# HGRN2 attention and a PReLU network on one core: a first step gated by batch, sooner keys, a wait inside the state increments, and a new hand-written order of work

## The chip, the cores and the metric

The kernel runs on one core of a Trainium2 chip. TensorE (PE) multiplies, with its weight loads listed apart (PEld); VectorE (DVE) and ScalarE (ACT) do the elementwise work, GpSimd (POOL) some setup, and SyncE (SP) issues most DMAs. PSUM takes the products, SBUF holds everything else. The metric is the device time of one execution, in microseconds.

## The reference

Two blocks, one after the other. First a gated linear attention: batch 4, 8 heads, 768 time steps, head size 48. The second block is a two-layer network with a PReLU between its layers: 3072 tokens (batch by time), 384 to 2048 to 384.

```
f = 1.0 / (1.0 + np.exp(-f_logit))
for t in range(S):
    state = f[:, :, t, :, None] * state + np.einsum('bhd,bhe->bhde', k[:, :, t], v[:, :, t])
    y[:, :, t] = np.einsum('bhd,bhde->bhe', q[:, :, t], state)
x = y.transpose(0, 2, 1, 3).reshape(B * S, H * D)
h = x @ w_in
g = np.maximum(h, 0.0) + alpha * np.minimum(h, 0.0)
out = g @ w_out
```

All of it is float32. Weights arrive as 64-bit words and are put together on the chip.

## The kernel before

**Steps.** The time axis is cut into 6 chunks of 128 and the batch into 2 pairs, so there are 12 steps (`steps`, L776): step n is chunk c = n // 2 of batch pair bp = n % 2. In a step a chunk's attention for two batches and eight heads is computed, and then the network for those 256 tokens. Only the state (kept in rows of `vs`) links the steps of a batch pair.

**Stages.** Each piece of work is a Python generator, one letter per kind. A line of text, `ORDER`, names which generator goes on next; each call to it issues instructions up to its next `yield`. `manual_schedule` (L784) keeps that order on PE, DVE, ACT and SP. POOL is not in that list. START writes the order out for the first part (until step 5), USUAL is repeated after that, with T S Y O for step n, P and K with a plus for step n + 1, and n for the network of step n - 1. `X:3` means three turns.

- P, `prepare` (L267), 8 turns: (1) loads of f, q, k and v (on POOL for steps 1 to 4, on SP for the others), (2) sigmoid on f and copies on ACT, (3) the products of decays kr and fs, and the lagged queries qd (`lagged`, L297), on DVE, (4) ACT's us copies; for later chunks two scans; for the first chunk q4 and k4 (L338, L364), (5) more decayed queries (for later chunks q4, k4 and the first of them), (6) and (7) keys decayed to the end of a block (`ended`, `keys`), transposed by DVE into kt, and queries decayed from its start, (8) ACT's A copies (L445).
- S and T, `scores` (L549) of batch 0 and 1 of the pair, 4 turns: first products on PE, masked copies on DVE (L572), second products (k4 by us) on PE, masked copies (L582).
- K, `keys_moved` (L449): 16 DMAs bring the transposed keys kt into ksn, 8 issued by SP and 8 by POOL.
- M, `landed` (L460): a small matmul that reads ksn, and so waits for these DMAs on PE. It writes into a network bank, which `network` then takes as its next ph (named pw; `early`, L658).
- O, `carry` (L466), 4 turns (8 in the first chunk): "off" products on PE (L495), ACT copies, the state increments on PE (L526, 64 matmuls of ksn by vs into the PSUM tile pairs[1]), and `moved(0)` on DVE (L536, L540), which brings the state on. The first chunk also has "half" products (L480), PE transposes for ksn and ACT copies.
- Y, `attend` (L601), 4 turns (5 in step 0): A copies on ACT (two turns, L606), the output products py on PE (L617), then y copies on ACT, `moved(1)` on DVE and ten DMAs into xT (step 0: products xt, L636, instead of DMAs).
- n, `network` (L653), 13 turns (12 in step 0): eight ph groups f0 to f7 (12 matmuls, a relu on ACT at L669 and two gates on DVE at L671; sums on DVE after f3 and f7), then the second layer in seven half-size products pa to pe (16 matmuls each): turn 9 has pa and pb, 10 pc and pd, 11 more of pa and pc, 12 pe and the store of o1, 13 the store of o0. Step 0 uses plain products po instead (turns 9 to 12).
- a, w: the eight pieces of w_in, upper part on ACT (two operations, and a load on SP) and the rest on DVE. b, g: the same for w_out. W: sums of the halves of w_out on DVE. i: a matmul on constants that fills a pause on PE. X: gives PSUM banks to the network.

**Buffers that matter.** f, q, k, us, k4, kt and ksn exist once, so a load waits until the last reader of the step before. pairs[0] and pairs[1] are two PSUM tiles of two banks, used by S, T, O and Y in turn; the network has four banks.

Of the kernel before, what the change touches and what calls it, by code (L numbers as in the profile page):

```python
# [8 lines left out]
F32 = mybir.dt.float32  # L9
# [5 lines left out]
AF = mybir.ActivationFunctionType  # L15
# [13 lines left out]

BEGUN = 5  # L30
START = (
# [7 lines left out]
)  # L39
USUAL = "T S T S n:4 T S P+ T S P+ n:2 Y M n O:4 n:2 P+ Y P+ Y P+ Y n:3 P+:3 K+ n"  # L40

LOOSE = ("a", "w", "b", "g", "W", "i", "X")

# [17 lines left out]
def kernel(  # L61
# [72 lines left out]
    def bank(name):  # L134
        return net["pool"].tile([128, 512], F32, tag="net", name=name)
# [131 lines left out]
    def prepare(bp, c, x):  # L267
# [5 lines left out]

        def load(name, src, bufs=2):
            t = work.tile([128, W], F32, tag=name, name=f"{name}_{i}", bufs=bufs)
            loads.dma_start(out=t.rearrange("p (u x) -> p u x", u=U),
                              in_=src[b0:b0 + U, c].rearrange("u p h t -> p u (h t)"))
            return t

        f = quads(load("f", fT, 1))  # L280
# [5 lines left out]
            loads.dma_start(out=vs[bp][t_, cc, :, 0:DM], in_=v[b0:b0 + U, c, t_].rearrange("u t d -> t u d"))  # L286
        yield

        nc.scalar.activation(f, f, AF.Sigmoid)
        nc.scalar.copy(kr[:, :, 2:3], f[:, :, 3:4])  # L290
        qdv = [qd[:, :, QO[d]:QO[d] + NB * (4 - d)].rearrange("p g (i r) -> p g i r", r=4 - d) for d in range(4)]
        nc.scalar.copy(qd[:, :, 0:DB], q.rearrange("p (g t) -> p g t", t=DB))
# [6 lines left out]
            nc.vector.tensor_tensor(qdv[d], last[:, :, :, 1:5 - d],  # L299
                                    f[:, :, 1:5 - d].rearrange("p (g i) r -> p g i r", i=NB), ALU.mult)  # L300

        nc.vector.tensor_tensor(kr[:, :, 1:2], f[:, :, 2:3], f[:, :, 3:4], ALU.mult)
        lagged(1)
        nc.vector.tensor_tensor(kr[:, :, 0:1], f[:, :, 1:2], kr[:, :, 1:2], ALU.mult)
        lagged(2)
        nc.vector.tensor_tensor(fq, f[:, :, 0:1].rearrange(by32, i=NB), kr[:, :, 0:1].rearrange(by32, i=NB), ALU.mult)
        lagged(3)
        yield


# [24 lines left out]
        if c:  # L335
            scans()
            yield
        nc.vector.tensor_tensor(q4, q4, f[:, :, 0:1].rearrange("p (g i) o -> p g i o", i=NB)  # L338
                                .broadcast_to((128, G, NB, 4)), ALU.mult)
        pre = ps[:, 0:NS - 1].rearrange("p (g i) -> p g i", i=NB + 1)  # L340
# [22 lines left out]
        k4 = x["k4"] = work.tile([128, W], F32, tag="k4", name=f"k4_{i}", bufs=1)  # L363
        nc.vector.tensor_tensor(k4, k, kr.rearrange("p n r -> p (n r)"), ALU.mult)  # L364
        if c:
            earlier(2)
        else:
# [92 lines left out]
    def landed(bp, c, x):  # L460
        to = early[steps[steps.index((bp, c)) - 1]] = bank(f"pw_{bp}_{c}")
        nc.tensor.matmul(to[:, 0:4], lhsT=ident, rhs=x["ksn"][:, 0, 0:128:32], start=True, stop=True,
                         skip_group_check=True)
        yield

    def carry(bp, c, x):  # L466

        i = f"{bp}_{c}"
        home = more if (bp, c) == steps[0] else pairs
        off = home[0]  # L470
        if not c:
            half = home[1]
            for u in range(U):
                for hp in range(HP):
                    for j in range(NJ):
                        g = (u * HP + hp) * NJ + j
                        o = (u * HP + hp) * 16
                        for par in range(2):
                            r_ = rows(par)
                            nc.tensor.matmul(half[DB * j:DB * (j + 1), par, o:o + 16], lhsT=x["k16"][r_, g],  # L480
                                             rhs=x["q16"][r_, g], start=True, stop=True)
# [36 lines left out]
        pd = home[1]  # L518
        ksn = x["ksn"]
        for u in range(U):  # L520
# [24 lines left out]
        yield  # L545
        moved(0)
        yield
# [105 lines left out]
    def network(bp, c, x):  # L653
# [1 line left out]
        xT = x["T"]  # L655
        plain = (bp, c) == steps[0]
        for f in range(NH):
            ph = early.pop((bp, c), None)  # L658
            if ph is None:
                ph = bank(f"ph{f}_{i}")  # L660
            tiles = (2 * f, 2 * f + 1) if plain else (f, f + NH)
            for kt in range(NK):
                for j, m in enumerate(tiles):
# [10 lines left out]
                sums(slice(f - 3, f + 1))  # L674
            yield

        def store(u, o):
            t0 = ((U * bp + u) * NC + c) * C
            nc.sync.dma_start(out=out[t0:t0 + C], in_=o)

        if plain:
            po = [bank(f"po{u}_{i}") for u in range(U)]
# [39 lines left out]
        product(pc, s3, t3, more=True)  # L722
        plus(o0[:, DH:DM], pd, u2)
        nc.scalar.activation(o0[:, 0:DH], pa[:, 0:DH], AF.Copy, scale=UP)
        yield
        pe = bank(f"pe_{i}")
        product(pe, s4, b22)
# [3 lines left out]
        store(1, o1)  # L731
        yield
        plus(o0[:, DH:DM], pe, o0[:, DH:DM])
        store(0, o0)
        yield

    late, early = {}, {}

    def sums(fs_):

# [43 lines left out]
    with tc.manual_schedule(engines={mybir.EngineType.PE, mybir.EngineType.DVE, mybir.EngineType.Activation,  # L784
                                     mybir.EngineType.SP}):
        run = {}
        for n, step in enumerate(steps):
            x = {}
            for key, stage_ in zip("POYKMn", (prepare, carry, attend, keys_moved, landed, network)):
# [59 lines left out]
```

## Time and profile before

| what | value |
|---|---|
| median of 3 executions | 616.25 us (614.02 to 617.06) |
| the profiled execution, its own time | 616.97 us |
| its span | 615.2 us |
| PE busy | 586.0 us |
| PEld busy | 523.2 us |
| DVE busy | 495.1 us |
| ACT busy | 243.6 us |
| POOL busy | 84.4 us |
| mean granted TensorE clock | 0.97 |

The span is the time from the first to the last instruction that the profile shows; 1.77 us of the profiled execution's time lie outside it. Busy time is summed over an engine's instructions, and a matmul's end is modelled, so a busy PE is a full queue and not PE at its peak. A view of waits lists what ended an engine's idle time; a chain of waits goes back from the last instruction to whatever released it. The granted clock is the share of TensorE's full clock that the throttle let through.

The costliest groups are the first layer's matmuls and the gate on DVE (line, engine, operation, output and inputs, count, busy us and mean ns, idle before):

```
L664 PE MATMUL ph<-xT,w_in_sb 128*128 128x256 f32 x1032 | 231.5, 382 | 0.0
L671 DVE SCALAR_TENSOR_TENSOR gate<-neg,om,ph 128x256 f32<-128x256 f32 x172 | 72.9, 478 | 37.8 <-ACT neg L669 37.8
```

### The profile page before, as it was taken

Reading aid. Unit: us, or ns where it says so; the run is one execution under the profiler, and the core shown is the slowest. Engines: PE = TensorE matmul, PEld = TensorE weight load, DVE = VectorE, ACT = ScalarE, POOL = GpSimd, SP = SyncE. Lnnn points to the kernel's source line nnn. Section 1 sums busy time; section 2 is a strip of 40 time slices with the busy share of each in tenths; the row PEclk is TensorE's granted clock in tenths of the full one; section 3 lists DMA queues with packets and bytes.
Section 4 is the critical chain, followed back from the end, with each engine's and each line's share of the span. In section 5 each row is a group of like instructions: output and inputs, shape, how many; then the busy total and the mean of one; then the engine's idle time right before and its main releaser. Section 6 shows DMA issues by size and latency. Waiting matters only on the chain.

```text
span 615.2 us, 18129 instructions
## 1 busy us (share of the span) xinstructions
PE 586.0 (95%) x7762; PEld 523.2 (85%) x7762; DVE 495.1 (80%) x997; ACT 243.6 (40%) x418; POOL 84.4 (14%) x162
## 2 busy tenths in 40 slices
PE   2689999999999699999999999999999999999997
PEld 1468857899899599899899899889889889889997
DVE  7869999999788679688988988988988986982351
ACT  4588863434431352342442442343343343231110
POOL 9110004004003001200200300200200200200000
PEclk7688999999999799999999999999999999999999
DMA  9937616114105301601601511501511511201000
GB/s 306 344 106 260 236 29 144 36 35 120 23 1 158 49 2 28 180 3 33 161 16 27 161 23 27 165 19 27 141 43 27 140 43 28 52 2 28 26 1 26
DMA packets 52720, 50.36 MB, mean 82 GB/s; under 512 B 26688, under 2 KB 43200, under 8 KB 52640
## 3 DMA queue, kind: packets, MB, share of 16 engines
q1 hardware_dynamic: 42624, 37.46, 20.6%
q0 software_dynamic: 5504, 9.90, 6.4%
q10 hardware_dynamic: 4512, 1.85, 1.3%
q8 instruction: 61, 1.00, 0.7%
q14 instruction: 19, 0.16, 0.1%
HBM read 36.21 MB, written 4.72 MB: 67 GB/s over the span
## 4 chain that ended last, share of the span: by engine, by line
PE 92%; DMA 2%; issue 2%; DVE 2%; ACT 1%; SPq 0%; DVEq 0%
PE ph L664 36%; PE pc L703 10%; PE pa L703 9%; PE pair L563 6%; PE pw L664 5%; PE pd L703 5%; PE pb L703 5%; PE pe L703 4%; PE pair L617 4%; PE po L684 3%; DMA k<-in_kT 1%; PE pair L526 1%; PE pair L495 1%; PE more L773 1%; PE xt L636 1%
## 5 line engine op out<-in xcount | busy, mean ns | idle before, releaser
L664 PE MATMUL ph<-xT,w_in_sb 128*128 128x256 f32 x1032 | 231.5, 382 | 0.0
L664 PEld LDWEIGHTS ph<-xT,w_in_sb 128*128 128x128 f32 x1032 | 193.9, 190 | 28.5 <-issue 1.7
L671 DVE SCALAR_TENSOR_TENSOR gate<-neg,om,ph 128x256 f32<-128x256 f32 x172 | 72.9, 478 | 37.8 <-ACT neg L669 37.8
L669 ACT ACTIVATE neg<-ph 128x512 f32<-128x512 f32 x86 | 50.1, 595 | 118.8 <-PE ph L664 78.0
L703 PE MATMUL pc<-t,S 128*128 128x192 f32 x352 | 61.5, 328 | 0.0
L703 PE MATMUL pa<-w_out_sb,gate 128*128 128x192 f32 x352 | 61.2, 327 | 0.0
L703 PEld LDWEIGHTS pa<-w_out_sb,gate 128*128 128x128 f32 x352 | 57.9, 190 | 0.8
L455 POOL DMA_DIRECT2D ksn<-kt x80 | 46.1, 584 | 87.8 <-DVE kt L407 62.0
L703 PEld LDWEIGHTS pc<-t,S 128*128 128x128 f32 x352 | 57.2, 190 | 0.6
L445 ACT COPY A<-q 48x512 f32<-48x512 f32 x44 | 27.2, 617 | 66.2 <-DVE q L393 65.8
L647 POOL DMA_DIRECT2D xT<-y x22 | 11.8, 543 | 286.7 <-ACT y L624 286.7
L572 DVE COPY_PREDICATED ad<-mraw,pair 128x256 f32<-128x256 int32 (+1 forms) x96 | 41.3, 451 | 5.2 <-PE pair L563 2.2
L582 DVE COPY_PREDICATED ad<-mquad,pair 128x224 f32<-128x224 int32 (+6 forms) x140 | 41.1, 299 | 4.2
L347 DVE TENSOR_TENSOR us<-us,fs 128x768 f32<-128x768 f32 (+5 forms) x60 | 37.0, 616 | 0.8
L707 DVE SCALAR_TENSOR_TENSOR Csum<-pc,Csum 128x192 f32<-128x192 f32 x22 | 7.9, 358 | 36.9 <-PE pc L703 36.6
L606 ACT COPY A<-ad 32x512 f32<-32x512 f32 x48 | 29.5, 615 | 10.8 <-DVE ad L582 10.4
L326 ACT COPY us<-qd 128x256 f32<-128x256 f32 x48 | 29.5, 673 | 10.6 <-DVE qd L299 10.3
L664 PE MATMUL pw<-xT,w_in_sb 128*128 128x256 f32 x120 | 31.0, 412 | 0.0
L748 DVE TENSOR_TENSOR S<-gate 128x512 f32<-128x512 f32 x44 | 30.3, 688 | 0.8
L703 PE MATMUL pe<-w_out_sb,S 128*128 128x192 f32 x176 | 30.5, 327 | 0.0
L703 PE MATMUL pb<-t,gate 128*128 128x192 f32 x176 | 30.4, 326 | 0.0
L703 PE MATMUL pd<-w_out_sb,S 128*128 128x192 f32 x176 | 30.4, 326 | 0.0
(125 smaller groups left out, 792.0 us busy)
## 6 DMA issues: line engine op xcount, KB each, us to landing
w_out_raw<-in_w_out SPq DMA_DIRECT2D x8, 767.8 KB, 5.9
w_in_raw<-in_w_in SPq DMA_DIRECT2D x8, 767.2 KB, 9.8
out<-o SPq DMA_DIRECT2D x24, 192.0 KB, 2.0
f<-in_fT SPq DMA_DIRECT2D x8, 512.0 KB, 3.9
q<-in_qT SPq DMA_DIRECT2D x8, 512.0 KB, 4.8
k<-in_kT SPq DMA_DIRECT2D x8, 512.0 KB, 6.5
vs<-in_v SPq DMA_DIRECT2D x16, 192.0 KB, 6.6
ksn<-kt SPq DMA_DIRECT2D x80, 32.0 KB, 2.2
```

The source lines that it names most:

```text
L326: nc.scalar.copy(q4[:, :, :, r], qdv[r][:, :, :, 0])
L347: nc.vector.tensor_tensor(us[:, :, UO[m]:UO[m] + 4 * n].rearrange("p g (i r) -> p g i r", r=4), us[:, :, skip:skip + 4 * n].rearrange("p g ...
L455: (nc.gpsimd if a % 2 else nc.sync).dma_start(out=ksn[32 * b:32 * (b + 1)].rearrange("p u (h x) -> p (u h) x", h=HP)[:, :, 32 * a:32 * a + n],
L563: nc.tensor.matmul(to[DB * j:DB * (j + 1), par, hp * step + lo:hp * step + hi], lhsT=keys[r_, g * DB:(g + 1) * DB], rhs=by[r_, g, lo:hi], ...
L572: nc.vector.copy_predicated(adu[:, :, :, d:4], mraw[:, d, :, d:4].bitcast(I32).unsqueeze(1).broadcast_to((128, H, NB, n)), rv[:, :, QO[d]: ...
L582: nc.vector.copy_predicated(ad[:, u, :, :, 4 * m:DB], mquad[:, lo:lo + n].bitcast(I32).unsqueeze(1).unsqueeze(1).broadcast_to((128, 2, HP, ...
L606: nc.scalar.copy(A[s_].rearrange("p u h t -> p (u h) t")[:, :, s_], ad[s_].rearrange("p u r h t -> p (u r h) t"))
L664: nc.tensor.matmul(ph[:, j * T:(j + 1) * T], lhsT=w_in_sb[:, kt, m * 128:(m + 1) * 128], rhs=xT[:, kt], start=(kt == 0 and j == 0), stop=( ...
L669: nc.scalar.activation(neg, phv, AF.Relu, scale=-1.0)
L671: nc.vector.scalar_tensor_tensor(gate[:, m % NH, m // NH], neg[:, j], om[:, m:m + 1], phv[:, j], ALU.mult, ALU.add)
L703: nc.tensor.matmul(to[:, 0:DH], lhsT=of(f), rhs=by(f), start=(f == 0 and not more), stop=(f == NH - 1), skip_group_check=True)
L748: nc.vector.tensor_tensor(to, x_, y_, op)
```

## The change

- In step 0, f is loaded in two DMAs, one per batch of the pair, and sigmoid and kr's first product are done in two halves. The lagged queries of step 0 come behind kr and fs instead of between them.
- k4 is computed ahead of q4, at the top of turn 4 or 5 of P, instead of after it.
- `landed` and `early` are gone. In `carry`, two small matmuls per later chunk (64 rows each, into four unused columns of pairs[1]) read ksn just ahead of the state increments.
- In the last step, the store of o0 is cut into two halves of the columns; the left half is issued in turn 11 of n, the right half in turn 13.
- START and USUAL are new. In USUAL, both first products stand together, py comes behind pc and pd, moved(0) behind the lags and scans of the next step, and the key moves one turn ahead of P's last.

```
--- before.py
+++ after.py
@@ -29,15 +29,15 @@
 
 BEGUN = 5
 START = (
-    "i P0 i P0:2 i P0:3 O0:2 a T0 P0 T0 i S0 i S0 i P1 T0 a P0 P1 O0 P1 O0 S0 T0 S0 i O0 P1 O0 S1 P1 Y0 i "
-    "O0:2 i Y0 w O1:2 Y0 S1 a Y0 X a S1 T1 a Y0 T1 w P2:2 T1 w P1 w:2 a:2 T1 w P1 S1 n0 a n0 b w:2 b g b "
-    "n0:2 O1 n0 O1 b P2 O1 g Y1 O1 n0:2 g n0 b Y1 S2 g P2 T2 b T2 n0 g:2 b S2 n0 g b g W O1 W P1 P2 n0 P2 "
-    "O1 Y1:2 P2 W n0 T2 S2 P3 S2 n1 P3 T2 Y2 K2 P3 n1 W n1 Y2 n1:2 O2 T3 n1 T3 M2 n1 W O2 n1 P3 S3 O2 S3 "
-    "O2 n1 P3 n1 P2 Y2 P3 n1 Y2 P4 P3 P4 P3 n1 S3 P4 T3 n1 n2 S3 n2:2 T3 Y3 n2 K3 n2:2 M3 n2 O3:2 P4 O3 "
-    "n2 O3 P4:2 n2:2 Y3:3 n2 S4 T4 P4 n2:2 T4 S4 n3 P5 K4 n3 P4 P5 S4:2 T4:2 n3 P5 M4 n3:4 O4 Y4 O4 Y4 "
-    "O4:2 n3 P5:2 n3:2 Y4 P5:2 Y4 n3:2 K5 n3 P5 "
+    "i P0:3 S0 i P0:2 T0 i O0:2 a i P0:2 P1 i T0 i:3 O0 T0 O0 P1 S0 P1 S0 O0 T0 S0 i w P0 i P1 O0 P1 O0 i "
+    "Y0:2 O0 a S1 Y0 O1 Y0 O1 X a S1 w Y0 T1 P2 T1 w a:2 w P1 n0 a:2 P1 w a w S1 P2 S1 n0 T1 w P1 w b "
+    "n0:2 T1 O1 b g O1 P2 b Y1 g n0 b n0 g O1 n0 b g b g n0 O1 P2 b:2 g n0 S2 P2 Y1 g:2 O1 S2 W P2 n0:2 "
+    "O1 P2 Y1:2 W n0 S2 W T2 P2 P3:2 S2 T2 W n1:2 T2 O2 T2 W P3 Y2 K2 n1 Y2 O2 n1:3 T3 S3:2 n1 T3 n1:2 "
+    "O2:2 P3:2 n1 Y2 P3 Y2 P3 n1 O3 n1 O3 S3 P4 T3 n1 P4 T3 P3 n2 S3 P4 Y3 n2 K3 Y3 n2:3 O3 P4 O3 n2 P4 "
+    "n2:2 Y3 n2 P4 n2 Y3 T4 P4 S4 T4 P5 S4 P4 n2:2 T4 S4 T4 S4 Y4 n2 n3:2 P5 n3:3 K4 Y4 O4:3 P5:2 O4 n3:3 "
+    "Y4 P5 n3:2 Y4 P5 n3 P5:2 n3 K5 n3 "
 )
-USUAL = "T S T S n:4 T S P+ T S P+ n:2 Y M n O:4 n:2 P+ Y P+ Y P+ Y n:3 P+:3 K+ n"
+USUAL = "S:2 T:2 n:3 P+ n S P+ T S n:3 T n Y n O P+ O P+ O Y n O P+ Y:2 n:2 P+:2 K+ n P+"
 
 LOOSE = ("a", "w", "b", "g", "W", "i", "X")
 
@@ -273,8 +273,10 @@
 
         def load(name, src, bufs=2):
             t = work.tile([128, W], F32, tag=name, name=f"{name}_{i}", bufs=bufs)
-            loads.dma_start(out=t.rearrange("p (u x) -> p u x", u=U),
-                              in_=src[b0:b0 + U, c].rearrange("u p h t -> p u (h t)"))
+            tu = t.rearrange("p (u x) -> p u x", u=U)
+            parts = [slice(u, u + 1) for u in range(U)] if name == "f" and not ahead else [slice(0, U)]
+            for p in parts:
+                loads.dma_start(out=tu[:, p], in_=src[b0:b0 + U, c].rearrange("u p h t -> p u (h t)")[:, p])
             return t
 
         f = quads(load("f", fT, 1))
@@ -286,7 +288,9 @@
             loads.dma_start(out=vs[bp][t_, cc, :, 0:DM], in_=v[b0:b0 + U, c, t_].rearrange("u t d -> t u d"))
         yield
 
-        nc.scalar.activation(f, f, AF.Sigmoid)
+        by_u = [slice(u * G * NB // U, (u + 1) * G * NB // U) for u in range(U)] if not ahead else [slice(0, G * NB)]
+        for p in by_u:
+            nc.scalar.activation(f[:, p], f[:, p], AF.Sigmoid)
         nc.scalar.copy(kr[:, :, 2:3], f[:, :, 3:4])
         qdv = [qd[:, :, QO[d]:QO[d] + NB * (4 - d)].rearrange("p g (i r) -> p g i r", r=4 - d) for d in range(4)]
         nc.scalar.copy(qd[:, :, 0:DB], q.rearrange("p (g t) -> p g t", t=DB))
@@ -299,12 +303,16 @@
             nc.vector.tensor_tensor(qdv[d], last[:, :, :, 1:5 - d],
                                     f[:, :, 1:5 - d].rearrange("p (g i) r -> p g i r", i=NB), ALU.mult)
 
-        nc.vector.tensor_tensor(kr[:, :, 1:2], f[:, :, 2:3], f[:, :, 3:4], ALU.mult)
-        lagged(1)
+        for p in by_u:
+            nc.vector.tensor_tensor(kr[:, p, 1:2], f[:, p, 2:3], f[:, p, 3:4], ALU.mult)
+        if ahead:
+            lagged(1)
         nc.vector.tensor_tensor(kr[:, :, 0:1], f[:, :, 1:2], kr[:, :, 1:2], ALU.mult)
-        lagged(2)
+        if ahead:
+            lagged(2)
         nc.vector.tensor_tensor(fq, f[:, :, 0:1].rearrange(by32, i=NB), kr[:, :, 0:1].rearrange(by32, i=NB), ALU.mult)
-        lagged(3)
+        for d in range(3 if ahead else 1, 4):
+            lagged(d)
         yield
 
 
@@ -335,6 +343,8 @@
         if c:
             scans()
             yield
+        k4 = x["k4"] = work.tile([128, W], F32, tag="k4", name=f"k4_{i}", bufs=1)
+        nc.vector.tensor_tensor(k4, k, kr.rearrange("p n r -> p (n r)"), ALU.mult)
         nc.vector.tensor_tensor(q4, q4, f[:, :, 0:1].rearrange("p (g i) o -> p g i o", i=NB)
                                 .broadcast_to((128, G, NB, 4)), ALU.mult)
         pre = ps[:, 0:NS - 1].rearrange("p (g i) -> p g i", i=NB + 1)
@@ -360,8 +370,6 @@
                 by = fq[:, :, 1:NB:NQ]
             nc.vector.tensor_tensor(to, of, by.unsqueeze(3).broadcast_to((128, G, 2, 4)), ALU.mult)
 
-        k4 = x["k4"] = work.tile([128, W], F32, tag="k4", name=f"k4_{i}", bufs=1)
-        nc.vector.tensor_tensor(k4, k, kr.rearrange("p n r -> p (n r)"), ALU.mult)
         if c:
             earlier(2)
         else:
@@ -457,12 +465,6 @@
                     in_=kt[32 * a:32 * (a + 1)].rearrange("p (g b x) -> p g b x", b=NJ, x=32)[:, :, b, 0:n])
         yield
 
-    def landed(bp, c, x):
-        to = early[steps[steps.index((bp, c)) - 1]] = bank(f"pw_{bp}_{c}")
-        nc.tensor.matmul(to[:, 0:4], lhsT=ident, rhs=x["ksn"][:, 0, 0:128:32], start=True, stop=True,
-                         skip_group_check=True)
-        yield
-
     def carry(bp, c, x):
 
         i = f"{bp}_{c}"
@@ -517,6 +519,10 @@
         yield
         pd = home[1]
         ksn = x["ksn"]
+        if c:
+            for par in range(2):
+                r_ = slice(64 * par, 64 * par + 64)
+                nc.tensor.matmul(pd[r_, par, 508:512], lhsT=ident[r_, r_], rhs=ksn[r_, 0, 0:128:32], start=True, stop=True)
         for u in range(U):
             for hp in range(HP):
                 for cc in range(NC2):
@@ -655,9 +661,7 @@
         xT = x["T"]
         plain = (bp, c) == steps[0]
         for f in range(NH):
-            ph = early.pop((bp, c), None)
-            if ph is None:
-                ph = bank(f"ph{f}_{i}")
+            ph = bank(f"ph{f}_{i}")
             tiles = (2 * f, 2 * f + 1) if plain else (f, f + NH)
             for kt in range(NK):
                 for j, m in enumerate(tiles):
@@ -674,9 +678,9 @@
                 sums(slice(f - 3, f + 1))
             yield
 
-        def store(u, o):
+        def store(u, o, d=slice(0, DM)):
             t0 = ((U * bp + u) * NC + c) * C
-            nc.sync.dma_start(out=out[t0:t0 + C], in_=o)
+            nc.sync.dma_start(out=out[t0:t0 + C, d], in_=o[:, d])
 
         if plain:
             po = [bank(f"po{u}_{i}") for u in range(U)]
@@ -722,6 +726,8 @@
         product(pc, s3, t3, more=True)
         plus(o0[:, DH:DM], pd, u2)
         nc.scalar.activation(o0[:, 0:DH], pa[:, 0:DH], AF.Copy, scale=UP)
+        if (bp, c) == steps[-1]:
+            store(0, o0, slice(0, DH))
         yield
         pe = bank(f"pe_{i}")
         product(pe, s4, b22)
@@ -731,10 +737,10 @@
         store(1, o1)
         yield
         plus(o0[:, DH:DM], pe, o0[:, DH:DM])
-        store(0, o0)
-        yield
-
-    late, early = {}, {}
+        store(0, o0, slice(DH, DM) if (bp, c) == steps[-1] else slice(0, DM))
+        yield
+
+    late = {}
 
     def sums(fs_):
 
@@ -786,7 +792,7 @@
         run = {}
         for n, step in enumerate(steps):
             x = {}
-            for key, stage_ in zip("POYKMn", (prepare, carry, attend, keys_moved, landed, network)):
+            for key, stage_ in zip("POYKn", (prepare, carry, attend, keys_moved, network)):
                 run[key, n] = stage_(*step, x)
             run["S", n], run["T", n] = (scores(u, *step, x) for u in range(U))
         for key in ORDER:
```

More of the change, by code (lines that the diff above doesn't have):

```diff
@@ L31 @@
 START = (
[7 rows of a table removed]
[7 rows of a table added]
 )
-USUAL = "T S T S n:4 T S P+ T S P+ n:2 Y M n O:4 n:2 P+ Y P+ Y P+ Y n:3 P+:3 K+ n"
+USUAL = "S:2 T:2 n:3 P+ n S P+ T S n:3 T n Y n O P+ O P+ O Y n O P+ Y:2 n:2 P+:2 K+ n P+"
 LOOSE = ("a", "w", "b", "g", "W", "i", "X")
@@ L275, in load @@
             t = work.tile([128, W], F32, tag=name, name=f"{name}_{i}", bufs=bufs)
-            loads.dma_start(out=t.rearrange("p (u x) -> p u x", u=U),
-                              in_=src[b0:b0 + U, c].rearrange("u p h t -> p u (h t)"))
+            tu = t.rearrange("p (u x) -> p u x", u=U)
+            parts = [slice(u, u + 1) for u in range(U)] if name == "f" and not ahead else [slice(0, U)]
+            for p in parts:
+                loads.dma_start(out=tu[:, p], in_=src[b0:b0 + U, c].rearrange("u p h t -> p u (h t)")[:, p])
             return t
@@ L287, in prepare @@
         yield
-        nc.scalar.activation(f, f, AF.Sigmoid)
+        by_u = [slice(u * G * NB // U, (u + 1) * G * NB // U) for u in range(U)] if not ahead else [slice(0, G * NB)]
+        for p in by_u:
+            nc.scalar.activation(f[:, p], f[:, p], AF.Sigmoid)
         nc.scalar.copy(kr[:, :, 2:3], f[:, :, 3:4])
@@ L300, in lagged @@
                                     f[:, :, 1:5 - d].rearrange("p (g i) r -> p g i r", i=NB), ALU.mult)
-        nc.vector.tensor_tensor(kr[:, :, 1:2], f[:, :, 2:3], f[:, :, 3:4], ALU.mult)
-        lagged(1)
+        for p in by_u:
+            nc.vector.tensor_tensor(kr[:, p, 1:2], f[:, p, 2:3], f[:, p, 3:4], ALU.mult)
+        if ahead:
+            lagged(1)
         nc.vector.tensor_tensor(kr[:, :, 0:1], f[:, :, 1:2], kr[:, :, 1:2], ALU.mult)
-        lagged(2)
+        if ahead:
+            lagged(2)
         nc.vector.tensor_tensor(fq, f[:, :, 0:1].rearrange(by32, i=NB), kr[:, :, 0:1].rearrange(by32, i=NB), ALU.mult)
-        lagged(3)
+        for d in range(3 if ahead else 1, 4):
+            lagged(d)
         yield
@@ L337, in prepare @@
             yield
+        k4 = x["k4"] = work.tile([128, W], F32, tag="k4", name=f"k4_{i}", bufs=1)
+        nc.vector.tensor_tensor(k4, k, kr.rearrange("p n r -> p (n r)"), ALU.mult)
         nc.vector.tensor_tensor(q4, q4, f[:, :, 0:1].rearrange("p (g i) o -> p g i o", i=NB)
@@ L361, in near @@
             nc.vector.tensor_tensor(to, of, by.unsqueeze(3).broadcast_to((128, G, 2, 4)), ALU.mult)
-        k4 = x["k4"] = work.tile([128, W], F32, tag="k4", name=f"k4_{i}", bufs=1)
-        nc.vector.tensor_tensor(k4, k, kr.rearrange("p n r -> p (n r)"), ALU.mult)
         if c:
@@ L458, in keys_moved @@
         yield
[L460 to L464, printed above, removed]
     def carry(bp, c, x):
@@ L519, in carry @@
         ksn = x["ksn"]
+        if c:
+            for par in range(2):
+                r_ = slice(64 * par, 64 * par + 64)
+                nc.tensor.matmul(pd[r_, par, 508:512], lhsT=ident[r_, r_], rhs=ksn[r_, 0, 0:128:32], start=True, stop=True)
         for u in range(U):
@@ L657, in network @@
         for f in range(NH):
-            ph = early.pop((bp, c), None)
-            if ph is None:
-                ph = bank(f"ph{f}_{i}")
+            ph = bank(f"ph{f}_{i}")
             tiles = (2 * f, 2 * f + 1) if plain else (f, f + NH)
@@ L675, in network, with store @@
             yield
-        def store(u, o):
+        def store(u, o, d=slice(0, DM)):
             t0 = ((U * bp + u) * NC + c) * C
-            nc.sync.dma_start(out=out[t0:t0 + C], in_=o)
+            nc.sync.dma_start(out=out[t0:t0 + C, d], in_=o[:, d])
         if plain:
@@ L724, in network @@
         nc.scalar.activation(o0[:, 0:DH], pa[:, 0:DH], AF.Copy, scale=UP)
+        if (bp, c) == steps[-1]:
+            store(0, o0, slice(0, DH))
         yield
@@ L733, in network @@
         plus(o0[:, DH:DM], pe, o0[:, DH:DM])
-        store(0, o0)
+        store(0, o0, slice(DH, DM) if (bp, c) == steps[-1] else slice(0, DM))
         yield
-    late, early = {}, {}
+    late = {}
     def sums(fs_):
@@ L788 @@
             x = {}
-            for key, stage_ in zip("POYKMn", (prepare, carry, attend, keys_moved, landed, network)):
+            for key, stage_ in zip("POYKn", (prepare, carry, attend, keys_moved, network)):
                 run[key, n] = stage_(*step, x)
```

14 rows, old and new, of the table START are left out of this document.

## The prediction

> **What bounds the kernel now.** I read the page's summary first, then busy time by stage, then the chain of waits, then the engines in order of time.
>
> ```profile
> span 615.2 us, 18129 instructions
> ...
> PE 586.0 (95%) x7762; PEld 523.2 (85%) x7762; DVE 495.1 (80%) x997; ACT 243.6 (40%) x418; POOL 84.4 (14%) x162
> ```
>
> TensorE is busy for 95% of the span. Cut at stage borders (columns: window, its length, then busy time of PE, PEld, DVE, ACT, POOL, granted clock, DMA share, GB/s):
>
> ```profile
> 0.00:51.00 51.00, 30.67 (x966) 23.20 (x966) 40.09 (x73) 29.89 (x51) 19.70 (x50) 0.73 0.77 258
> 51.00:101.00 50.00, 50.00 (x595) 37.16 (x584) 47.34 (x85) 35.29 (x55) 4.45 (x7) 1.00 0.50 164
> 101.00:202.00 101.00, 101.00 (x1298) 92.08 (x1287) 91.32 (x188) 39.54 (x69) 19.34 (x33) 1.00 0.27 67
> 202.00:265.00 63.00, 58.13 (x666) 52.10 (x665) 46.03 (x95) 21.08 (x37) 5.68 (x10) 0.95 0.23 56
> 265.00:572.00 307.00, 306.99 (x4056) 282.18 (x4055) 255.85 (x529) 112.37 (x198) 35.19 (x62) 1.00 0.23 59
> ```
>
> PE has no hole in 51 to 202 and 265 to 572. A new order can gain only in the first 51 us (step 0's attention, a chain through DVE, ACT and PE), at one hole after 202, and in the tail. In the steady part a step lasts 46.62 us (pw starts at 311.96 and 358.58), all PE. The chain of waits shows the hole (start, length, what):
>
> ```profile
> 194.84 8.61 DMA k<-in_kT
> ...
> 203.47 0.58 SPq L455
> ...
> 204.75 1.96 DMA ksn<-kt
> ...
> 207.56 0.56 PE pw L462 x2
> 208.13 5.33 PE pw L664 x12
> ```
>
> SP issued step 5's loads (P5) just ahead of step 4's key moves (K4, L455), the moves queued behind 1.9 MB, and the landing matmul L462 waited. Among PE's waits it is the longest after the start:
>
> ```profile
> PE more L480 <- DVE us L375: 9.8, 1, 9.8
> PE pw L462 <- DMA ksn<-kt: 4.9, 1, 4.9
> PE pair L563 <- issue: 4.4, 2, 2.6
> ```
>
> "Issue" names gaps that no semaphore explains, in mid-product: 2.57, 2.24, 0.85 and 1.80 us at 19.3, 26.5, 40.5 and 43.6, 7.46 in all.
>
> **The change, part by part.**
>
> **The hole at 202.** It costs 4.87 us idle; then 12 pw matmuls took 5.33 instead of 2.69 at a granted clock of 0.69 and 0.62: 2.64 more; 7.5 with the slower landing matmul. In the new order P5's loads stand after S4's first products, some 8 us before the end of product pe of step 2 (pa and pc 5.4, pe 2.6), so their 8.6 us are over by then. K4 is behind them and behind the two stores of n2. From the end of pe (e): T4's and S4's masked copies on DVE must go first (some 1 + 4.5 us), then plus and store (0.9), then 8 issues on SP at 0.68 us (5.47 in the steady part), landing 2.2 us: e + 14.1. PE comes to the state increments after 1.8 (T4, S4) + five ph groups at 2.64 + 0.6 (off) = e + 15.6. It fits by 1.5 us; issues at the loaded 1.04 us would miss by 1.4. I take **-7.5**; bounds -7.9 and 0.
>
> [...]
>
> **The start.** First ph begins at 51.04. Removed from its path: one sigmoid of 1.07 us after the whole f has landed (3.86) becomes two, the first under the second half's landing. A half costs 0.55 by half the row, at most 0.67 by the 128x256 copy, and one more SP issue (0.45) goes ahead of q and k; k then lands at 8.0, before its use at 8.9. kr's two halves cost 2 x 0.42 instead of 0.73. The lags move behind kr and fs, and k4 (1.15) runs where DVE stood waiting for ACT's us copies. Together DVE is some 1.3 us early at k16; but k16 also needs POOL's memset L321, which ends at 12.81, so the half products start at about 13.8 instead of 14.84. Both first products now stand before them, so DVE's first masks run unbroken from 19.1 to 22.5 instead of 20.42 to 24.80. Step 1's lags follow (3.7), then the second masks: 28.1 instead of 31.06. ACT has step 1's us copies behind it by then, so the A copies (2 x 1.24) and the carry copies (0.96) run on: py starts at 31.6 instead of 38.79. With py 2.2, y copies 1.1, xt 4.5 at the cold clock and T1's products 1.2 the first ph would start at 41.0. That has no issue gap. Of the 7.46 us before, some 5 moved the end (2.2 via the off copies, 0.85 in py, 1.8 in front of xt); I add 5: 46.0, so **-5.0**. Bounds 0 (every gap bites and ACT's queue as well) and -10 (none).
>
> [...]
>
> **Work moved behind the first ph.** S1's and T1's second products (0.9 + 0.75) now follow it; T2's second products (0.9) leave the stretch before step 1's network. **+0.75**. PE is full there, so this is paid.
>
> **ACT and DVE in the next 50 us.** DVE is busy 47.34 of 50, ACT 35.29. The order puts a.6 to a.8, P2's sigmoid and copies (2.7) and b.1 between the first relus; counting ACT's rows (1.7 a weight piece, 0.6 a relu, 1.24 two A copies) relu 6 ends near 25 after the first ph, where PE wants its bank at 24.3 for po. **+1.5**; bounds 0 and 3.
>
> **The steady step.** PE's work is the same: 46.62 less nothing. The two 64-row landing matmuls replace one 128-row pass of 0.16 us (0.11 before pw and 0.05 in it); the trace has none of this shape, so bounds are -0.16 and, at four weight loads and matmuls fully exposed at 0.1 each, +0.25 a step, -1.6 to +2.5 over ten. Nearest are the increments, 64 in 0.72 us, so I take 0. Behind the wait on PE now queue the increments, pc, pd and py; kt is ready 1.7 us into the step and PE arrives at 30.3, so it holds nobody in the steady part.
> What is tighter is py: moved(0) now stands on DVE behind T's second masks, f7's gate, the sums, all lags and the scans. From the end of f6, PE reaches py after 2.64 + 5.20 (pa, pb) + 0.62 + 0.16 + 0.72 + 2.80 (pc) + 2.60 (pd) = 14.74. DVE, by the spacing of such rows (these give sums and lags):
>
> ```profile
> 367.03 0.69 DVE L748 TENSOR_TENSOR S<-gate 128x512 f32<-128x512 f32 x1
> ...
> 369.56 0.63 DVE L302 TENSOR_TENSOR kr<-f 128x256 f32<-128x256 f32 x1
> ...
> 373.23 0.77 DVE L332 TENSOR_TENSOR_SCAN ps<-fs,ones 128x289 f32<-128x289 f32 x1
> ```
>
> needs 0.73 (relu) + 0.87 (gate) + 2.25 (masks) + 0.91 (gate) + 2.53 (sums) + 3.67 (lags) + 1.32 (scans) + 0.40 (plus) + 2.14 (moved) + 0.1 = 14.92: a wait of 0.2 us in each of steps 5 to 10, **+1.2**; bounds 0 and 5. py's turn later is harmless to the next ph: y copies, ten moves and landing end some 6.2 us after py, and PE has 5.4 + 2.8 + 1.5 = 9.7 us of other work.
> Keys moved ahead of q4 in P (k4, L364) shift nothing on PE.
>
> **The tail.** The last store carries 96 KB instead of 192. It took 2.0 us; the 48 KB moves of xT took 2.1, so size hardly counts: **-0.2**; bounds 0 and -0.5. The early half is issued 5 us before, under pe.
>
> **Sum:** -7.5 - 5.0 + 0.75 + 1.5 + 0 + 1.2 - 0.2 = -9.25. The profiled execution took 616.97 (615.2 is its span, 1.77 lie around it): 607.7. It stands 0.72 above the median of 616.25, so I give **607.0**.
>
> **Rivals.**
> 1. *The start runs without issue gaps and ACT keeps up.* For it: fewer products stand in bursts while the weights load, and the PE waits elsewhere anyway. Against: the same DMA load of 0.77 in the first 51 us. 607.0 - 5 - 1.5 = 600.5.
> 2. *K4's landing still holds PE.* The wait comes back inside the increments, because K4 is still behind P5 and now behind two stores. For: only 1.5 us to spare. Against: the loads are done by then. 607.0 + 7.5 = 614.5 in full.
> 3. *The start gains nothing*, because ACT's longer queue in front of py takes it back: 607.0 + 5 = 612.0.
> 4. *The other side: DVE sets the step.* One place: moved(0) in front of py. DVE is busy 41.22 us of a 46.6 us step. f5's gate ends 1.7 us before f6's relu; lateness of DVE beyond that adds one for one to py's wait. 4.0 us late makes the wait 2.5: six steps at 2.3 more, +13.8, 620.8. It turns slower than before from a wait of 0.2 + 9.25/6 = 1.7 us a step. For: DVE has 95% in 51 to 101 and 90% in 101 to 202. Against: in steady rows DVE waits 1.08 us for f7's relu and 2.51 for pc, so it catches up twice a step.
>
> **Chances.** Forecast 0.54 (its own range 603 to 611), rival 1 0.14, rival 2 0.12, rival 3 0.11, rival 4 0.09. What a measurement can tell from no change is 0.5%, that is 613.2 to 619.3. The forecast, rivals 1 and 3 and a third of rival 2 (a partial wait) are faster: 0.83; the rest of rival 2, 0.08, is the same; rival 4, 0.09, slower. The range runs from rival 1's 600.5 with 1 us for its size to rival 2 with 1 us: 599.5 to 615.5; it leaves out rival 4 and a little at either end.
>
> **What would show it.** The first ph near 46 instead of 51; no PE wait above 1 us on ksn and a granted clock of 1.0 after 60; a steady step of 46.6 to 46.9 with waits of PE at L617 on DVE vs (L540) of some 0.2 us; a short PE wait at the first po. Wrong it would be if the first ph stays at 51, if the landing matmuls in the increments wait for microseconds, or if py waits over 1.7 us a step.

## The result, and the profile after

The changed kernel takes 609.02 us (median of 4 runs, 608.84 to 609.72) beside 616.65 for the kernel before in the same runs: a ratio of 0.9885, with a 95% interval of 0.9853 to 0.9917. The forecast was 607.0. Its profiled execution has a span of 607.1 us, 8.1 less than before.

The summary and the busy time by stage of the changed kernel, in the windows used before (length, busy time of PE, PEld, DVE, ACT, POOL, granted clock, DMA share, GB/s):

```profile
span 607.1 us, 18178 instructions
...
PE 583.9 (96%) x7786; PEld 521.8 (86%) x7786; DVE 495.0 (82%) x998; ACT 242.3 (40%) x419; POOL 85.4 (14%) x162
```

```profile
0.00:51.00 51.00, 33.09 (x929) 25.73 (x930) 42.00 (x77) 32.91 (x56) 20.55 (x50) 0.93 0.81 252
51.00:101.00 50.00, 49.66 (x583) 36.69 (x582) 49.00 (x90) 37.91 (x59) 7.79 (x14) 1.00 0.51 166
...
202.00:265.00 63.00, 62.80 (x737) 57.30 (x739) 51.65 (x105) 21.48 (x37) 5.70 (x10) 1.00 0.20 52
265.00:572.00 307.00, 305.49 (x4032) 280.61 (x4023) 249.92 (x515) 107.82 (x194) 35.30 (x62) 1.00 0.23 60
```

The hole after 202 is filled (62.80 of 63 busy, clock 1.00). In the long steady window PE now shows 1.5 us of gaps where it had none. PE's waits, longest first:

```profile
PE pair L569 <- ACT us L334: 6.0, 1, 6.0
PE more L532 <- ACT ksn L518: 5.0, 1, 5.0
...
PE more L482 <- issue: 1.9, 1, 1.9
PE pair L525 <- issue: 1.7, 8, 0.2
```

The wait of 4.9 us on the key moves is gone. Two waits in step 0 lead the list now (6.0 and 5.0 us), and the landing pair (L525) has a gap of 0.2 us in each of eight steps that the view puts down to "issue". One step's increments in PE's order of time (start, length, what, idle before):

```profile
358.85 0.69 PE L497 MATMUL pair<-q,kh 48*64 48x64 f32 x32
359.46 0.25 PE L525 MATMUL pair<-ksn,ident 64*64 64x4 f32 x2
359.93 0.19 PE L525 MATMUL pair<-ksn,ident 64*64 64x4 f32 x1 [0.23 <-issue]
359.94 0.25 PE L532 MATMUL pair<-vs,ksn 64*48 64x48 f32 x3
```

Points of both chains of waits cut the span into stretches, and these account for all of it:

| stretch | before | after | difference |
|---|---|---|---|
| start to step 0's first ph | 51.11 | 45.16 | -5.95 |
| to step 1's first ph | 50.05 | 51.53 | +1.48 |
| to step 4's first ph, with the hole | 146.35 | 139.82 | -6.53 |
| to step 11's first ph, seven steps | 324.81 | 328.44 | +3.63 |
| to the end of the last pe | 38.93 | 38.93 | 0 |
| the tail | 3.95 | 3.22 | -0.73 |

So the start and the hole gave 12.5 us, and almost 4 went back in the steady part, where a step went from 46.62 to 47.15 us.

### The profile page after: what moved, and what is told of

The parts are those of the page before. It is cut to its first block, busy times and chain, and to the rows that moved or that the text cites. A ratio compares the mean times of both kernels' runs of the same rounds, so it can differ in the third digit from the quotient of the medians.

```text
span 607.1 us, 18178 instructions
## 1 busy us (share of the span) xinstructions
PE 583.9 (96%) x7786; PEld 521.8 (86%) x7786; DVE 495.0 (82%) x998; ACT 242.3 (40%) x419; POOL 85.4 (14%) x162
## 3 DMA queue, kind: packets, MB, share of 16 engines
q10 hardware_dynamic: 4512, 1.85, 1.3%
## 4 chain that ended last, share of the span: by engine, by line
PE 92%; ACT 1%; issue 1%; DMA 1%; SPq 0%; DVE 0%; ACTq 0%; DVEq 0%
PE ph L668 42%; PE pa L707 10%; PE pc L707 9%; PE pair L569 6%; PE pe L707 5%; PE pd L707 4%; PE pb L707 4%; PE pair L623 4%; PE po L688 3%; PE pair L532 1%; PE pair L497 1%; DMA xT<-y 1%; PE pair L525 1%; PE xt L642 0%; ACT us L334 0%
## 5 line engine op out<-in xcount | busy, mean ns | idle before, releaser
L668 PE MATMUL ph<-xT,w_in_sb 128*128 128x256 f32 x1152 | 255.7, 381 | 0.0
L668 PEld LDWEIGHTS ph<-xT,w_in_sb 128*128 128x128 f32 x1152 | 216.7, 190 | 31.5 <-issue 1.4
L675 DVE SCALAR_TENSOR_TENSOR gate<-neg,om,ph 128x256 f32<-128x256 f32 x192 | 81.9, 479 | 40.0 <-ACT neg L673 39.8
L673 ACT ACTIVATE neg<-ph 128x512 f32<-128x512 f32 x96 | 56.3, 595 | 115.6 <-PE ph L668 76.9
L630 ACT COPY y<-pair 128x512 f32<-128x512 f32 x22 | 11.8, 589 | 46.4 <-PE pair L623 45.8
L707 PEld LDWEIGHTS pe<-w_out_sb,S 128*128 128x128 f32 x176 | 28.9, 190 | 0.1
```

Source lines behind the costliest of these rows:

```text
L668: nc.tensor.matmul(ph[:, j * T:(j + 1) * T], lhsT=w_in_sb[:, kt, m * 128:(m + 1) * 128], rhs=xT[:, kt], start=(kt == 0 and j == 0), stop=( ...
L673: nc.scalar.activation(neg, phv, AF.Relu, scale=-1.0)
L675: nc.vector.scalar_tensor_tensor(gate[:, m % NH, m // NH], neg[:, j], om[:, m:m + 1], phv[:, j], ALU.mult, ALU.add)
L707: nc.tensor.matmul(to[:, 0:DH], lhsT=of(f), rhs=by(f), start=(f == 0 and not more), stop=(f == NH - 1), skip_group_check=True)
```

## The experiments

Three questions: what lengthens the step, what filled the hole, and what sets the start.

**Landing as before, ahead of f7** (from step 5 on):

```
-USUAL = "... n:3 T n Y n O P+ O ..."
+USUAL = "... n:3 T M n Y n O P+ O ..."
+    def landed(bp, c, x): (as in the kernel before; carry has the pair only for steps 2 to 4)
```

> From step 5 on the landing matmul is again one 128-row pass into a network bank, placed ahead of f7. In the changed kernel off and increments take 1.39 us from the end of off's products to the end of the increments, against 0.72 + 0.16 before, so a step is 47.14 instead of 46.62. Waits theory (eight semaphore waits of 51 ns on PE's sequencer stand behind only 0.62 us of off products and show; behind a long group they are hidden): the step falls by 0.5 to some 46.65, and the whole by 7 x 0.5 = 3.5 us against the changed kernel's 609.0: 605.5. Shape theory (four small passes with their own weight loads cost the time): the same here. If the step lengthens because of py instead (moved(0) late on DVE), nothing changes: 609.0.

Measured: a step of 46.69 us, 0.46 less; span 604.0. The runs spread over 605.78 to 609.05 (median 608.48), ratio to the kernel before 0.9872 (0.9828 to 0.9916). The step moved as both theories of the landing said and not as the py theory said; the median did not reach 605.5. The traced run came near it (605.78, first ph at 45.28 beside 45.16 in the changed kernel). That the others started later is likely, since the start spreads by microseconds between the traces of this case (below), but it is not shown.

**The same pair ahead of the off products** (from step 5 on):

```
         q3, ks, kh, f64 = (x[n] for n in ("q3", "ks", "kh", "f64"))
+        if steps.index((bp, c)) >= 5:
+            for par in range(2):
+                r_ = slice(64 * par, 64 * par + 64)
+                nc.tensor.matmul(home[1][r_, par, 508:512], lhsT=ident[r_, r_], rhs=x["ksn"][r_, 0, 0:128:32], start=True, stop=True)
```

> From step 5 on the same two 64-row landing matmuls stand ahead of the off products, behind pb's 2.6 us, instead of behind off. Waits theory: the eight waits pass while pb runs, the step falls by some 0.4 us (the 0.17 and 0.23 of issue), 7 x 0.4 = 2.8: 606.2. Shape theory: the same four passes cost the same, 609.0.

Measured: 605.99 (605.11 to 607.54), ratio 0.983 (0.979 to 0.987); a step of 46.57 us, 0.58 less than in the changed kernel and no longer than before the change. PE's order of time in that kernel:

```profile
357.60 2.76 PE L712 MATMUL pb<-t,gate 128*128 128x192 f32 x16
360.29 0.22 PE L494 MATMUL pair<-ksn,ident 64*64 64x4 f32 x2
360.31 0.27 PE L502 MATMUL pair<-q,kh 48*64 48x64 f32 x2
360.37 0.20 PE L494 MATMUL pair<-ksn,ident 64*64 64x4 f32 x2
```

The same four small passes follow pb without a gap and run among the off products. This decides for the waits: shape and count are the same. The semaphore waits of the seven steps, which in the changed kernel are 56, eight each, now stand behind the 2.76 us of pb and not behind the 0.69 us of off.

**One 128-row matmul in the place of the two:**

```
-            for par in range(2):
-                r_ = slice(64 * par, 64 * par + 64)
-                nc.tensor.matmul(pd[r_, par, 508:512], lhsT=ident[r_, r_], rhs=ksn[r_, 0, 0:128:32], start=True, stop=True)
+            nc.tensor.matmul(pd[:, 0, 508:512], lhsT=ident, rhs=ksn[:, 0, 0:128:32], start=True, stop=True)
```

> One 128-row landing matmul in the place of the two 64-row ones, in all later chunks. Waits theory: as many waits in the same place, at most 0.1 us a step less: 608 to 609. Shape theory: two passes instead of four, some 0.3 us a step less, over ten steps 3: 606.

Measured: 611.81 (610.12 to 613.01), a step of 47.31 to 47.35 us at first, 0.2 longer, and of 47.53 to 47.81 in the last three, of which two also hold a wait of pe for ACT (0.21 and 0.43 us). Neither theory had it longer; the shape theory falls. The gap in front grew from 0.23 to 0.34 us, the pass is 0.35 instead of 0.25 long. Why a full-width pass shows more of the wait was not followed further.

**No landing matmul at all** (the three lines and their `if` removed):

> No landing matmul: the state increments wait for the key moves themselves. Waits theory: the waits stand in the same place on PE's sequencer, spread over the first increments, and only the passes' own time goes, 0.1 to 0.2 us a step: 607 to 608. Shape theory: the whole 0.5 us a step goes, over ten steps 5: 604.

Measured: 609.33 (609.05 to 610.5), a step of 47.08, 0.07 less. The waits stay with the first increments. The instructions of that line show them (PEldq is the sequencer of PEld; count, then duration in ns, least, median and most):

```profile
L528 PE MATMUL pair<-vs,ksn x704: 202/205/241, 78.3 to 550.9; 64*48 64x48 f32 x176
L528 PEldq EVENT_SEMAPHORE  x81: 51/51/51, 26.8 to 550.1; - x81
```

In the changed kernel the landing line has 79 of these, some 8 a step, 8 x 51 ns = 0.4 us. That is the size of what the place costs. The kernel before had 89 of them at its landing line (L462), behind a ph group of 2.7 us, and showed no gap there but the one in the hole; in one of its steps nine of them stand at 354.4 to 355.3, while ph groups fill PE from 353.01, and the landing matmul follows these without a gap at 358.30.

**The old order under the new code** (START and USUAL of before, without M):

> The changed kernel's code (f by batch, k4 first, landing pair in the increments, split store) with the old START and USUAL, less the turns of M. If the order carries the gain: the hole at step 4 is back (7.5 us) in front of the increments instead of pw, the first ph is at 50 to 51, since POOL's memset of us sets the half products anyway, and the landing pair costs up to 0.5 a step over ten steps: 615 to 621, no better than before. If the code edits carry it: first ph 2 us or more earlier and 612 or below.

Measured: 612.8 (612.4 to 613.37), ratio 0.9934 (0.9914 to 0.9954). First ph at 50.2, step 47.15, as expected, but no hole: PE has no wait on the key moves, although step 5's loads are again just ahead of them. That part was missed: the wait itself stands four ph groups later here, inside the increments. The time lies between the two forecasts. So the new order was worth some 4 us (609.0 against 612.8): 5.0 in the start, less 1.25 from there to step 4's first ph (191.35 instead of 190.10), and the hole was not its doing. Which part of the new order gives the start was not taken apart, and some of the 5.0 may be the start's own spread: k landed 9.0 us after its issue here and 6.9 in the changed kernel. The next two put that to the test.

**New order, step 4's landing at its old place:**

```
-    ... Y4 n2 n3:2 P5 n3:3 K4 Y4 O4:3 ...
+    ... Y4 n2 K4 n3:2 P5 n3 M4 n3:2 Y4 O4:3 ...
```

> The changed kernel with its new order, but step 4's landing matmul in the old form and place: ahead of the fourth ph group of step 3's network, instead of inside the increments after five groups and off. All other steps keep the pair. Theory A (the new order keeps step 5's loads out of the key moves' way, so they land in time): no wait at the landing, 609. Theory B (the hole went because the wait stands later, and the new order lands the keys hardly sooner): in the changed kernel the last key move lands near 203.6, 12.1 us after that network's first ph; PE gets to the landing after three groups, 7.9 us, waits some 4 us, then runs cold for 2 to 3: 615 to 616.

Measured: 616.67 (614.65 to 618.74), ratio 0.9992 (0.9965 to 1.0019), the whole gain gone. The chain of waits of this kernel:

```profile
198.60 0.27 DVE o L719
...
198.92 0.36 SPq L691
...
204.22 1.96 DMA ksn<-kt
...
206.84 0.56 PE pw L470 x2
207.41 4.88 PE pw L676 x12
```

PE waited 4.03 us and then ran 12 matmuls in 4.88 instead of 2.69. From step 0's first ph to step 4's this execution takes 197.27 us, 5.9 more than the changed kernel; the rest of what it loses is a late start (first ph at 49.08). What held the keys now was no load: the last store of o0 waits for DVE's masked copies, and the moves wait behind it on SP. Counted from the first ph of step 3's network, the new order does land the keys sooner, 11.4 us after it (206.18 - 194.78) instead of 14.0 (206.71 - 192.74). But PE also comes to the landing sooner, 8.03 us after it instead of 9.95, so most of the wait stays: 4.03 of 4.87 us.

**The kernel before, with only step 4's wait moved** into the increments (M4 dropped, the pair for step 4 alone):

> The kernel before the change, its order, code and landing matmuls kept, with one difference: step 4 has no landing matmul ahead of pw, but the pair inside its state increments, four ph groups later. If the place of the wait alone makes or fills the hole: keys land near 206.7, PE comes to the increments near 214, no wait, no cold stretch, 7.5 us less and 0.5 for the pair's own cost: 609 to 610, about as much as the whole change. If the new order was needed for it: 615 to 617.

Measured: 609.12 (608.12 to 612.2), ratio 0.9871 (0.9829 to 0.9914). No wait on the keys is left; PE runs through to the pair, and the view shows no idle time in front of it:

```profile
202.81 13.22 PE L668 MATMUL ph<-xT,w_in_sb 128*128 128x256 f32 x60
215.96 0.69 PE L495 MATMUL pair<-q,kh 48*64 48x64 f32 x32
216.57 0.25 PE L523 MATMUL pair<-ksn,ident 64*64 64x4 f32 x2
```

From step 0's first ph (54.12) to step 4's (242.75) it takes 188.6 us instead of 196.4: 7.8 less. The span is 610.4 only because this execution's start is 3 us late. With the last experiment this shows the cause: the hole is a matter of where the wait stands. This one edit brings the kernel before as far as the whole change does (609.12 beside 609.02).

**f and the last store in one piece:**

```
-            parts = [slice(u, u + 1) for u in range(U)] if name == "f" and not ahead else [slice(0, U)]
+            parts = [slice(0, U)]
...
-        if (bp, c) == steps[-1]:
-            store(0, o0, slice(0, DH))
```

> f of step 0 in one load and one sigmoid again, and the last store in one. First theory: the half products wait for POOL's memset of us (L329, over at 13.65 in the changed kernel), DVE stood idle 1.5 us for it, so f in one piece costs nothing at the half products: they start at 15.1 as in the changed kernel, first ph 45.1. Rival: f by halves carries a part of the start, first ph 45.6 or later. The tail from the last pe to the end grows from 3.2 to some 3.9 us. Together 609.7 against 609.0.

Measured: 610.42 (610.03 to 611.31). The half products start at 15.98 instead of 15.12 and the first ph is at 46.15, which is the rival's outcome. But the first theory's chain still stands in this trace: DVE waits 1.50 us for the memset as in the changed kernel, and what moved is POOL, which waits 0.79 us for the load of om and begins its mask copies at 6.40 instead of 5.54. Whether f in one piece delays that load, or the start only varied, one trace does not show; it is a hint at 1 us and no more. The tail is 3.72 us from the last pe's end, so the halved store is worth 0.5 (3.72 - 3.22).

**POOL's mask copies behind its memsets** (the three loops of copies into mhalf, dense and mquad moved into a generator that runs after step 0's turn 5):

> POOL's mask copies (mhalf, mquad) and the copies into dense come after its memsets for step 0's us tile instead of ahead of them. If the memset holds k16: DVE's 1.5 us idle in front of L380 goes, the half products start at some 13.6 instead of 15.1 and the first ph comes up to 1.5 us earlier: 607.5 to 609. If DVE's and ACT's later chain (the wait of 2.2 us for step 1's sigmoid) sets the first ph, it stays at 45.1: 609.0.

Measured: 609.94 (609.24 to 612.06). DVE's wait for POOL is gone (the operation runs at 13.08 instead of 13.68), the half products start at 14.79, but the first ph is at 46.44. The gain is used up inside the half products: their mid-product gap is 2.69 us instead of 1.87, so their second part starts at 18.56 instead of 18.05, and DVE then waits 3.49 us for step 1's sigmoid instead of 2.17.

**Three idle matmuls fewer** ahead of step 0's off:

```
-    "... a i P0:2 P1 i T0 i:3 O0 T0 ..."
+    "... a i P0:2 P1 i T0 O0 T0 ..."
```

> Three of the idle matmuls between step 0's first masks and its off products left out (2.7 of the 4.5 us that PE spends on them at 18.6 to 23.0). Theory: they stand in front of off, off releases ACT's A copies, and these stand in front of step 1's sigmoid, for which DVE waits 2.17 us; without them off runs at 20.4 and the first ph comes 2 us earlier: 607. Rival: they hold the granted clock at 1.00; without them it falls to the 0.5 to 0.7 of the kernel before, xt takes 4.5 us instead of 2.8, and the first ph comes no earlier: 609 to 611.

Measured: 608.23 (607.6 to 608.61). Both theories held in part, one after the other. In the changed kernel ten passes of idle matmuls stand between the half products and off:

```profile
18.05 0.62 PE L482 MATMUL more<-us 48*32 48x16 f32 x40 [1.87 <-issue]
18.60 4.49 PE L779 MATMUL more<-ones 128*128 128x256 f32 x10
23.02 0.69 PE L497 MATMUL more<-q,kh 48*64 48x64 f32 x32
```

Without six of them off runs at 21.08 instead of 23.02 and py starts at 33.48 instead of 36.50, and then the clock is low for xt:

```profile
36.42 1.15 PE L482 MATMUL pair<-us 48*32 48x16 f32 x100
39.79 0.33 PE L482 MATMUL pair<-us 48*32 48x16 f32 x28 [2.22 <-issue]
40.05 4.54 PE L642 MATMUL xt<-y,dense 128*128 128x256 f32 x12
45.37 2.86 PE L668 MATMUL ph<-xT,w_in_sb 128*128 128x256 f32 x12
```

xt takes 4.54 us instead of 2.86, at a granted clock of 0.66 in 40 to 45, and the first ph stands where it was, at 45.4. PE was busy for 1.78 of the 4 us before, at a granted clock of 1.00: here the clock fell behind a stretch that was only half filled, with a longest gap of 2.2 us. The last experiment has a stretch much like it (2.25 of 4 us, a gap of 1.75) and its xt took 2.86 us, so what made the clock fall is not shown.

**A combination: pair ahead of off, POOL's copies late, step 0's k loaded from ACT's queue:**

```
-                loads.dma_start(out=tu[:, p], ...
+                (nc.scalar if name == "k" and not ahead else loads).dma_start(out=tu[:, p], ...
```

> Landing pair ahead of off from step 5 on (as in the second experiment), POOL's mask copies behind its memsets, and step 0's k loaded from ACT's queue instead of third on SP's. Theory: a step of 46.6 instead of 47.15 (-3.5 to -4), k lands 0.5 to 2 us earlier and neither k nor POOL holds the half products, which start at 13.6 to 14 instead of 15.1 (-1): 604 to 605. If the later chain over off and step 1's sigmoid sets the first ph in any case, only the step: 605.5.

Measured: 607.79 (605.38 to 609.35), span 603.6 in the profiled run. k4 runs at 9.08 and the half products start at 14.01, a step takes 46.57, but the first ph is at 45.86. The traced run (605.38) is the second outcome; the median lies 2.3 us above it. The half products lose their 1.1 us at once: their mid-product gap is 2.99 us instead of 1.87, so their second part starts at 18.08, where it did in the changed kernel (18.05), and the idle matmuls, off and step 1's sigmoid follow as late as there. DVE only waits longer for that sigmoid, 3.62 us instead of 2.17.

**And with three idle matmuls fewer:**

> The kernel before this one, with three idle matmuls fewer ahead of step 0's off. If off and py now come earlier and the clock holds through xt (2.8 us): 2 us less than that kernel, 602 to 603. If the clock is low at xt again (4.5 us, as with the idles alone removed): no gain, 604 to 605.5.

Measured: 604.43 (603.1 to 605.98), ratio 0.9774 (0.973 to 0.9818). The first ph is at 43.48, xt takes 2.86 and the span is 601.3. Beside the kernel with the idle matmuls alone removed, the first ph is 1.96 us earlier, 1.68 of it in xt (2.86 instead of 4.54); off runs at 20.80 instead of 21.08, so the earlier half products add little. The granted clock was 0.77 in 30 to 40 and 1.00 in 40 to 50, although PE was busy for only 2.25 us of the 4 before 40, with a gap of 1.75 us. The forecast for a clock that holds was 602 to 603; the median lies 1.4 above it. One trace of each kernel does not show that this clock is the kernel's doing and not the execution's. It is the fastest version found, about 1.1% under the changed kernel by the two ratios (0.9774 / 0.9885 = 0.989) and 0.75% by the two medians (604.43 against 609.02).

## Why the prediction was near, point by point

- **The bound** was read rightly: PE sets the time, the gain could come only from start, hole and tail, and it did.
- **The hole, -7.5.** The size was right: 7.8 in the kernel with only the wait moved. The step's reasoning was half right. It named as the cure that P5's loads are over by then. What it then computed, keys against PE's arrival, was sound: it gave a margin of 1.5 us, and the last move went out at 200.9 and landed some 2.2 later, with PE there at 205.2, a margin of 2.1. But that arrival was already the later place of the wait, and the runs show that the place alone did it; with the wait at its old place the new order left a wait of 4.03 us behind masks and store.
- **The start, -5.0.** Measured -5.95. Inside, the working was off in both directions. The half products started at 15.12, not 13.8: 0.84 of it because POOL's memset was over at 13.65, not 12.81, behind mask copies that took 6.55 us instead of 4.62, the rest because the two DVE operations between memset and products take 1.44 us (13.68 to 15.12; 1.45 in the kernel before) where the working allowed 1.0. k landed at 9.0 in this execution and not at 8.0, and later in others (last section). The terms listed from py on add up to 40.6 and not to the 41.0 the working goes on with. py came at 36.5, not 31.6 plus gaps, since ten passes of idle matmuls (4.49 us), counted at nothing, stood in front of off and so of step 1's sigmoid. In return xt was taken at the cold clock of the kernel before (4.54 us at a granted 0.63) and took 2.86 us at 1.00, and the gaps in mid-product came to 3.9 us (1.87, 0.39, 1.63), where the forecast added 5. That these errors nearly cancel is luck.
- **Behind the first ph, 0.75 + 1.5.** Measured +1.48 together, but not as forecast: PE has no wait at the first po. The forecast's 0.75 for the moved products and one gap of 0.34 us make up 1.1 of it; the rest was not taken apart.
- **The landing pair, 0.** This is the term that was mis-sized: +0.5 us in each steady step, 3.6 us over the seven to step 11's first ph, and some 5 in all if steps 2 to 4 pay the same (an estimate), where the forecast took 0 and bounded it at +2.5. It priced passes and weight loads. By the experiments the cost is that of eight semaphore waits on PE's sequencer, 8 x 51 ns = 0.4 us: with them behind the 2.76 us of pb a step took 46.57 us, behind the 0.69 us of off 47.15.
- **py behind moved(0), +1.2.** Measured 0.08 a step (2.10 instead of 2.02), 0.5 in all. The balance of 14.92 against 14.74 was close: moved(0)'s last operation ends at 366.32, pd at 366.33. It is as close with the pair ahead of off, where PE comes sooner: 367.19 and 367.20, and py takes 2.10 to 2.11 again. So the wait that was forecast did not come, and the landing pair's time is not what hid it.
- **The tail, -0.2.** Measured -0.73 beside the kernel before and -0.5 by the whole store. The 96 KB store landed 1.6 us after issue, the 192 KB one 1.9.

The sum was 2 us off by the medians (the profiled times moved 8.08 us and not 9.25), with the landing pair's 5 us partly made good by start, py, tail and the work behind the first ph. So the sizes of hole and start were right in the main, and that the number came so near is in part luck. DVE never set the step, and the rival without issue gaps did not come either: they came to 3.9 us.

## What to carry to other kernels

A wait on an engine that sets the time has a place, and here the place was worth as much as the whole reordering: 609.12 us with step 4's wait alone moved, 609.02 with the whole change. Two places paid: later, just ahead of the first reader (188.6 us instead of 196.4 from step 0's first ph to step 4's), and directly behind a long group (a step of 46.57 us with the wait behind pb's 2.76 us, 47.15 with it behind off's 0.69). In the kernel before, the rows without idle time ahead of the landing matmul said only that the work in front was long enough: with off in front, 0.2 us of gap showed in each of eight steps. Filler matmuls held back what stood behind them (off ran at 23.02 with ten passes in front and at 21.08 with four), but with four xt took 4.54 us in one kernel and 2.86 in another; before they are taken out or put in, both the chain they delay and the granted clock behind them have to be looked at. And an earlier start is worth nothing when a gap behind it grows by as much (half products at 14.01 instead of 15.12, their gap 2.99 us instead of 1.87, their second part at 18.08 instead of 18.05), so the row behind the gap is the one to compare.

## What was not expected of the hardware

- POOL's 13 small mask copies took 1.85 + 0.83 us where DVE waited for q at that time (second experiment, DVE busy 4.78 of 7 us in 5 to 12), 2.53 + 2.09 in the kernel before (5.58 of 7), and 3.06 + 3.49 us in the changed kernel (6.70 of 7). In these three traces the copies took longer the more DVE was busy beside them; why is not shown. That the DVE work moved forward delayed the very memset it then waited for (over at 13.65 us instead of 12.81) is the author's reading of them; the memset itself took 0.21 us in all three.
- The same code has a start that varies: among the executions with an unchanged step 0, the first ph was at 45.2 to 49.1, and k landed 6.9 to 9.0 us after its issue in the five whose views show it. These rank the same by both (6.9, 7.2, 7.3, 8.4, 9.0 us beside 45.16, 45.28, 45.94, 47.83, 48.28); the sixth, with the first ph at 49.08, is also the last to run k4 (at 11.59, the others at 9.12 to 11.24). So the loads of the start are where its spread should be looked for; no run held them fixed. Before the change k took 5.8, issued 0.4 us earlier, and was needed one operation later.
